# GpSimd instead of VectorE inverts the sums of the later softmaxes, by a power

## The chip, the cores and the metric

The kernel runs on one core of a Trainium2 chip. TensorE multiplies matrices, VectorE, ScalarE and GpSimd work on elements, SyncE starts the DMAs. The metric is the device time of one execution in microseconds, the median of three runs.

## What is computed

Two attentions over the same q, k and v (batch 4, 8 heads, 576 tokens, 64 dimensions), added, and then two feed-forward layers over all 2304 tokens. The first attention works on q, k and v averaged over four tokens ("pooled"); the second lets each token see only the tokens less than four away. Both normalise by a softmax, and it is the denominator of these that the change touches.

```python
def sm_attn(qq, kk, vv):
    s = scale * np.matmul(qq, kk.transpose(0, 1, 3, 2))
    a = np.exp(s - np.max(s, axis=-1, keepdims=True))
    a = a / (np.sum(a, axis=-1, keepdims=True) + 1e-09)
    return np.matmul(a, vv)
# q_d, k_d, v_d: means over 4 tokens;  scores outside |i - j| < 4: -1e9
x = np.repeat(sm_attn(q_d, k_d, v_d), 4, axis=2) + local_attention(q, k, v)
h = x @ w_in;   x = (np.maximum(h, 0) ** 2) @ w_out
h = x @ w_in2;  out = (h * np.cos(h)) @ w_out2
```

## The kernel before

The tokens are cut into 40 windows of 56 to 60 queries, ten for each batch, and the windows are worked on in pairs: pair 0 holds windows 0 and 1, pair 19 the last two. A pair has two softmaxes, one for each parity of the heads, each on a tile of 128 rows by 4 x 64 scores. Eight windows (four pairs) make a block of some 460 tokens, and there are five blocks. Beside them the pooled attention has one softmax for each batch and head pair (`down`, 96 rows by 3 x 144).

A first phase, in which `early[0]` is true, does what the first block needs: pairs 0 to 3 and the pooled attention of batch 0. Then layer 1 runs block by block over 16 slots of 128 hidden units. A slot is a stage A (`stage_a`, L830: 12 matmuls of the block's 460 columns into the one bank `ps_h`), the relu, square and split of h into a high part gh and a low part gl (ScalarE L854, L855, L842, VectorE L848), and a stage B (`stage_b1`, L913: 12 matmuls that add to four banks `acc`). At a block's end the four banks are copied to y (L951, L953). The attention of the following pairs runs between the slots, so that the block's input is there when the block begins; so does the conversion of the weights from 64-bit numbers (`split`, L675 to L716; its subtraction of the high part L711 and that of the sums L801 are GpSimd's). Layer 2 (L865, L937) follows behind layer 1, with nothing of the attention in it.

A pair's way behind the first phase: score matmuls (L573, in the order's rows with the masks of L554), the maximum on VectorE, the exponential on ScalarE (L392 with the sums beside it, or L406 and then a VectorE sum, L408), then the two steps of this change: the small constant is added to the sums (L498, VectorE) and they are inverted (L499, VectorE). GpSimd multiplies the scores by that (L500), TensorE transposes them (L512), ScalarE copies the transposed tile, TensorE multiplies with v (L615), VectorE adds the pooled attention (L632), ScalarE makes the high part xh (L644) and VectorE the low part xl (L646) of the block's input, which stage A reads. In `down` the two steps are L428 and L431, GpSimd's product is L432, and its transpositions, product with v and copy are L442, L458 and L466. Each engine executes its own instructions strictly in the order in which they stand.

What sets that order: the program's text is recorded with its dependencies, and a scheduler that plans with its own costs of instructions puts each engine's instructions in a row (`schedule_with_timeline_sim`). A changed instruction can so move others on all engines. A few places are pinned with `behind(...)` and with a high priority for the relu's helper.

Of the kernel before, what the change touches and what calls it, by code (L numbers as in the profile page):

```python
# [8 lines left out]
F32 = mybir.dt.float32  # L9
# [5 lines left out]
ALU = mybir.AluOpType  # L15
# [4 lines left out]
P = 128  # L20
B, H, S, D = 4, 8, 576, 64
FACTOR = 4
# [72 lines left out]
def kernel(  # L95
# [11 lines left out]
    nc = tc.nc  # L107
    weights = {1: w1.bitcast(U32), 2: w2.bitcast(U32)}

    const = ctx.enter_context(tc.tile_pool(name="const", bufs=1))  # L110
# [23 lines left out]
        nc.vector.memset(t, v)  # L134
    down_half = const.tile([P, 1], F32, name="down_half")
    nc.vector.memset(down_half, 1.0 / 64 - 0.5)
    half_pi = const.tile([P, 1], F32, name="half_pi")
    nc.vector.memset(half_pi, math.pi / 2)

# [12 lines left out]
    early = [True]  # L152
# [22 lines left out]
    def done(name, n=1):  # L175
        f = taken[name].pop(0) if early[0] and name in SPREAD else None
        if f is None:
            used[name] -= n
        elif f in caps:
            used[f] -= n  # L180
        else:
            spare.append(f)
# [51 lines left out]
    def done_a(*ts):  # L234
        for t in ts:
            if t is not None:
                used[kinds.pop(id(t))[0]] -= 1
# [147 lines left out]
    def exps(bank, sv, mx, pr, scale, apiece):  # L385
# [21 lines left out]
        yield  # L407
        nc.vector.tensor_reduce(out=mx[:, 1], in_=pr, op=ALU.add, axis=AX.X)  # L408

    def down(b, hp):  # L410
        while b not in pooled:
            yield
        _, kp, vp = pooled[b]
        if b not in xds:
            xds[b] = cm.tile([P, HPAIR, SD], F32, tag="xd", name="xd")
        yield from need("dpr")
        s, = yield from need_a()
        sv = s[:QROWS, :3 * SD].rearrange("r (m s) -> r m s", m=3)
        qf = qp[:, hp].rearrange("p a s -> p (a s)")
        for m in range(3):  # L420
            last["pe"] = nc.tensor.matmul(sv[:, m], qf[:, m * QROWS:(m + 1) * QROWS], kp[:, hp], start=True, stop=True).ins  # L421
        qk_used[b] = qk_used.get(b, 0) + 1
        if qk_used[b] == HPAIR:
            done("qp")
        mx = cm.tile([QROWS, 2, 3], F32, tag="dmx", name="dmx", bufs=4)
        pr = task_tile("dpr", QROWS, 3 * SD).rearrange("p (m s) -> p m s", m=3)
        yield from exps(s, sv, mx, pr, SCALE / FACTOR ** 2, b < 2)
        nc.vector.tensor_scalar(  # L428
            out=mx[:, 1], in0=mx[:, 1], scalar1=1e-9, scalar2=float(FACTOR), op0=ALU.add, op1=ALU.mult
        )  # L430
        nc.vector.reciprocal(out=mx[:, 1], in_=mx[:, 1])  # L431
        nc.gpsimd.tensor_tensor(  # L432
            out=pr, in0=pr, in1=mx[:, 1].unsqueeze(2).broadcast_to([QROWS, 3, SD]), op=ALU.mult
        )
        yield
        if not early[0]:
            yield
        yield from need("dpt")
        tps = yield from need_a(2)
        for kt in range(2):  # L440
            for m in range(3):
                last["pe"] = nc.tensor.transpose(  # L442
                    tps[kt][:KTOK, m * QROWS:(m + 1) * QROWS], pr[:, m, kt * KTOK:(kt + 1) * KTOK],
                    ident[:QROWS, :QROWS],
                ).ins
        done("dpr")
        pt = task_tile("dpt", KTOK, 4 * SD).rearrange("p (k s) -> p k s", k=2)
        for kt in range(2):
            nc.scalar.copy(out=pt[:, kt], in_=tps[kt][:KTOK, :2 * SD])
        done_a(*tps)  # L450
        yield
        while early[0] and "vp" not in bands:
            yield
        av, = yield from need_a()
        for kt in range(2):
            for a in range(2):
                rows = slice(a * D, (a + 1) * D)
                last["pe"] = nc.tensor.matmul(  # L458
                    av[rows, :SD], vp[:, kt, hp * P + a * D:hp * P + (a + 1) * D], pt[:, kt, a * SD:(a + 1) * SD],
                    start=kt == 0, stop=kt == 1,  # L460
                ).ins
        done("dpt")
        vp_used[b] = vp_used.get(b, 0) + 1
        if vp_used[b] == HPAIR:
            done("vp")
        last["xd"] = nc.scalar.copy(out=xds[b][:, hp], in_=av[:, :SD]).ins  # L466
        done_a(av)
        downs.add((b, hp))
# [13 lines left out]
    def soft(s, sv, pr_tag, pr, q, a, pts):  # L482
        apart = early[0]
        mx = cm.tile([P, 2, HPAIR], F32, tag="mx", name="mx", bufs=8)
        if 2 * q >= DVE_MASK:
            at = [mask_at(w) for w in (2 * q, 2 * q + 1)]
            for i in range(2) if at[0] != at[1] else (slice(0, 2),):
                i = slice(2 * i, 2 * i + 2) if isinstance(i, int) else slice(0, HPAIR)
                nc.vector.tensor_tensor(
                    out=pr[:, i], in0=sv[:, i], op=ALU.add,  # L490
                    in1=const_sb[:, at[i.start // 2]:at[i.start // 2] + WK].unsqueeze(1).broadcast_to(
                        [P, i.stop - i.start, WK]
                    ),
# [1 line left out]
            done_a(s)  # L495
            s, sv = None, pr
        yield from exps(s, sv, mx, pr, SCALE, a == 0 if apart else 2 * q < W0[2])
        nc.vector.tensor_scalar_add(out=mx[:, 1], in0=mx[:, 1], scalar1=1e-9)  # L498
        nc.vector.reciprocal(out=mx[:, 1], in_=mx[:, 1])  # L499
        last["pr"] = (nc.vector if early[0] else nc.gpsimd).tensor_tensor(  # L500
            out=pr, in0=pr, in1=mx[:, 1].unsqueeze(2).broadcast_to([P, HPAIR, WK]), op=ALU.mult
        ).ins
# [811 lines left out]
```

## Time and profile before

| what | us |
|---|---|
| median of three runs | 913.27 (912.74 to 913.54) |
| the profiled execution, own time | 909.99 |
| its span, first to last instruction | 908.2 |
| TensorE busy | 888.2 |
| VectorE busy | 643.1 |
| ScalarE busy | 575.0 |
| GpSimd busy | 96.2 |

TensorE's time stands in two rows, PE for matmuls and PEld for the loads of weights that run beside them. Matmuls are pipelined and their ends are modelled, so a busy PE is not necessarily at its peak; the distance from one start to the next is the safer reading. A wait is put down to what ended it last.

### The profile page before, as it was taken

Reading aid. Unit: us, or ns where it says so; the run is one execution under the profiler, and the core shown is the slowest. Engines: PE = TensorE matmul, PEld = TensorE weight load, DVE = VectorE, ACT = ScalarE, POOL = GpSimd, SP = SyncE. Lnnn points to the kernel's source line nnn. Section 1 sums busy time; section 2 is a strip of 40 time slices with the busy share of each in tenths; the row PEclk is TensorE's granted clock in tenths of the full one; section 3 lists DMA queues with packets and bytes.
Section 4 is the critical chain, followed back from the end, with each engine's and each line's share of the span. In section 5 each row is a group of like instructions: output and inputs, shape, how many; then the busy total and the mean of one; then the engine's idle time right before and its main releaser. Section 6 shows DMA issues by size and latency. Waiting matters only on the chain.

```text
span 908.2 us, 17806 instructions
## 1 busy us (share of the span) xinstructions
PE 888.2 (98%) x6962; PEld 811.2 (89%) x6962; DVE 643.1 (71%) x1265; ACT 575.0 (63%) x1041; POOL 96.2 (11%) x79
## 2 busy tenths in 40 slices
PE   7889999999999999999999999999999999999997
PEld 5678778888888987889999999999999999999997
DVE  7899997567666665563311187988888897879786
ACT  5778776455655555454534477777777677767774
POOL 2001310122203322222200000000000000000000
PEclk9799999999999999999999999999999999999999
DMA  9499878967889766884897966655666666566673
GB/s 283 175 326 332 307 279 288 329 246 253 291 315 311 262 232 207 292 308 173 287 388 244 355 226 204 204 191 190 207 201 203 199 204 199 190 198 209 208 228 105
DMA packets 72904, 223.57 MB, mean 246 GB/s; under 512 B 9620, under 2 KB 14612, under 8 KB 68724
## 3 DMA queue, kind: packets, MB, share of 16 engines
q1 hardware_dynamic: 72820, 222.43, 71.7%
q8 instruction: 55, 0.90, 0.4%
q14 instruction: 29, 0.24, 0.1%
HBM read 181.50 MB, written 40.89 MB: 245 GB/s over the span
## 4 chain that ended last, share of the span: by engine, by line
PE 87%; DVE 5%; DMA 4%; ACT 3%; issue 1%; POOL 0%; DVEq 0%; SPq 0%; ACTq 0%
PE ps_h L865 23%; PE ps_h L830 19%; PE acc L913 19%; PE acc L937 18%; DMA raw<-in_w_dram 2%; DMA pl<-in_pool_v_dram 2%; PE ps_a L615 1%; PE ps_warm L1050 1%; DVE bits L695 1%; PE ps_a L573 1%; PE ps_a L458 1%; PE acc L935 1%; PE ps_a L512 1%; PE ps_a L421 1%; ACT bits L675 1%
## 5 line engine op out<-in xcount | busy, mean ns | idle before, releaser
L865 PE MATMUL ps_h<-x,w2hi 128*128 128x256 f32 x1152 | 161.8, 283 | 0.0
L848 DVE TENSOR_TENSOR gl<-gt,gh 128x460 fp32r<-128x460 f32 (+1 forms) x80 | 58.2, 728 | 142.4 <-ACT gh L842 85.2
L865 PEld LDWEIGHTS ps_h<-x,w2hi 128*128 128x128 f32 x1152 | 148.1, 191 | 0.1
L937 PE MATMUL acc<-bl,gh 128*128 128x256 f32 x504 | 139.2, 277 | 0.0
L830 PE MATMUL ps_h<-xh,w1hi 128*128 128x460 f32 (+3 forms) x324 | 122.7, 380 | 3.7 <-ACT gt L854 3.5
L913 PE MATMUL acc<-gl,w1hi 128*128 128x460 f32 (+1 forms) x320 | 120.0, 375 | 0.0
L830 PE MATMUL ps_h<-xl,w1hi 128*128 128x460 f32 (+3 forms) x324 | 118.8, 368 | 0.0
L913 PE MATMUL acc<-gh,w1hi 128*128 128x460 f32 (+1 forms) x320 | 105.5, 374 | 0.8 <-ACT y L951 0.8
L854 ACT ACTIVATE gt<-ps_h 128x460 f32<-128x460 f32 (+1 forms) x80 | 44.1, 552 | 96.9 <-PE ps_h L830 96.7
L913 PE MATMUL acc<-gh,lo 128*128 128x460 f32 (+1 forms) x256 | 94.9, 371 | 0.0
L937 PEld LDWEIGHTS acc<-bl,gh 128*128 128x128 f32 x504 | 94.7, 188 | 0.0
L905 DVE TENSOR_TENSOR gl<-g,gh 128x896 fp32r<-128x896 f32 x72 | 78.2, 1087 | 10.7 <-ACT gh L900 10.6
L937 PE MATMUL acc<-w2hi,gh 128*128 128x256 f32 x288 | 79.8, 277 | 0.0
L937 PE MATMUL acc<-w2hi,gl 128*128 128x256 f32 x288 | 79.4, 277 | 0.0
L873 ACT ACTIVATE u<-ps_h,quarter 128x512 f32<-128x512 f32 x72 | 49.3, 685 | 46.6 <-PE ps_h L865 46.3
L880 DVE SCALAR_TENSOR_TENSOR r<-u,ps_h 128x512 f32<-128x512 f32 x72 | 49.4, 686 | 38.8 <-PE acc L937 22.3
L900 ACT ACTIVATE gh<-g 128x896 fp32r<-128x896 f32 x72 | 68.1, 945 | 11.2 <-DVE g L898 11.2
L885 ACT ACTIVATE r<-r,half_pi 128x512 f32<-128x512 f32 x72 | 51.8, 719 | 34.2 <-DVE r L881 34.2
L830 PEld LDWEIGHTS ps_h<-xh,w1hi 128*128 128x128 f32 x324 | 60.8, 188 | 13.3 <-ACT gt L854 5.8
L865 PE MATMUL ps_h<-x,w2lo 128*128 128x256 f32 x432 | 68.5, 281 | 0.0
L830 PEld LDWEIGHTS ps_h<-xl,w1hi 128*128 128x128 f32 x324 | 60.9, 188 | 5.9 <-issue 0.2
L913 PEld LDWEIGHTS acc<-gh,w1hi 128*128 128x128 f32 x320 | 59.4, 188 | 7.6 <-ACT y L951 0.9
(150 smaller groups left out, 1911.4 us busy)
## 6 DMA issues: line engine op xcount, KB each, us to landing
bl<-wo_d SPq DMA_DIRECT2D x70, 896.0 KB
raw<-in_w_dram SPq DMA_DIRECT2D x32, 1024.0 KB
lo<-lo_d SPq DMA_DIRECT2D x128, 256.0 KB
qkw<-in_win_qk_dram SPq DMA_DIRECT2D x16, 512.0 KB
pl<-in_pool_qk_dram SPq DMA_DIRECT2D x24, 288.0 KB
wo_d<-raw SPq DMA_DIRECT2D x16, 384.0 KB
out_dram<-o SPq DMA_DIRECT2D x18, 256.0 KB
vw<-in_win_v_dram SPq DMA_DIRECT2D x16, 256.0 KB
```

What stands on the lines that cost most here:

```text
L421: last["pe"] = nc.tensor.matmul(sv[:, m], qf[:, m * QROWS:(m + 1) * QROWS], kp[:, hp], start=True, stop=True).ins
L830: nc.tensor.matmul(h[:, t0:t1], a[:, c * P:(c + 1) * P], x[:, c, t0:t1], start=i == 0, stop=i == len(order) - 1)
L848: last["gl"] = nc.vector.tensor_tensor(out=gl, in0=gt, in1=gh.bitcast(F32), op=ALU.subtract).ins
L854: last["relu"] = nc.scalar.activation(out=gt, in_=h, func=AF.Relu).ins
L865: nc.tensor.matmul(h[:, s * TB:(s + 1) * TB], a[:, c * P:(c + 1) * P], x[:, c], start=i == 0, stop=i == len(order) - 1,)
L873: nc.scalar.activation(out=u, in_=h, func=AF.Identity, bias=quarter, scale=float(1.0 / (2 * math.pi)))
L880: nc.vector.scalar_tensor_tensor(out=r, in0=u, scalar=-PI2_HI, in1=hv, op0=ALU.mult, op1=ALU.add)
L885: nc.scalar.activation(out=r, in_=r, func=AF.Sin, bias=half_pi, scale=1.0)
L900: nc.scalar.activation(out=gh, in_=g[:, 1:], func=AF.Copy)
L905: nc.vector.tensor_tensor(out=gl, in0=g[:, 1:], in1=gh.bitcast(F32), op=ALU.subtract)
L913: nc.tensor.matmul(acc[d][:, :n], a, x, start=f == 0 and i == 0, stop=f == NF - 1 and i == 2)
L937: nc.tensor.matmul(o, a[:, x], b, start=opens and i == 0, stop=p == NP2 - 1 and i == 2 and (k % 2 == 1 or k == NPROD - 1),)
```

## The change

Behind the first phase, the addition of 1e-9 (with the factor 4 in `down`, one in the windows) and the inversion are GpSimd's: a tensor-scalar instruction, and then a power with the exponent from a new constant tile of -1. In the first phase both stay on VectorE as before. It concerns 32 softmaxes of the windows and 12 of the pooled attention, 88 instructions.

```diff
+    minus_one = const.tile([P, 1], F32, name="minus_one")
+    nc.vector.memset(minus_one, -1.0)
...
+    def inverse(t, times):
+        if early[0]:
+            nc.vector.tensor_scalar(out=t, in0=t, scalar1=1e-9, scalar2=times, op0=ALU.add, op1=ALU.mult)
+            nc.vector.reciprocal(out=t, in_=t)
+            return
+        nc.gpsimd.tensor_scalar(out=t, in0=t, scalar1=1e-9, scalar2=times, op0=ALU.add, op1=ALU.mult)
+        nc.gpsimd.tensor_tensor(
+            out=t, in0=t, in1=minus_one[:t.shape[0]].broadcast_to([t.shape[0], t.shape[1]]), op=ALU.pow
+        )
...
         yield from exps(s, sv, mx, pr, SCALE / FACTOR ** 2, b < 2)
-        nc.vector.tensor_scalar(
-            out=mx[:, 1], in0=mx[:, 1], scalar1=1e-9, scalar2=float(FACTOR), op0=ALU.add, op1=ALU.mult
-        )
-        nc.vector.reciprocal(out=mx[:, 1], in_=mx[:, 1])
+        inverse(mx[:, 1], float(FACTOR))
...
         yield from exps(s, sv, mx, pr, SCALE, a == 0 if apart else 2 * q < W0[2])
-        nc.vector.tensor_scalar_add(out=mx[:, 1], in0=mx[:, 1], scalar1=1e-9)
-        nc.vector.reciprocal(out=mx[:, 1], in_=mx[:, 1])
+        inverse(mx[:, 1], 1.0)
```

The lines of the changed kernel behind it stand two to ten higher: L848 of before is L856 there, L500 is L508, L830 is L838, L913 is L921.

The first place is pair 4, the first behind the first phase. VectorE, before; `mx` holds the sums, `bits` the weight being converted:

```order
L498 TENSOR_SCALAR mx<-mx 128x4
L693 TENSOR_SCALAR bits<-bits 128x1024
L499 RECIPROCAL mx<-mx 128x4
L848 TENSOR_TENSOR gl<-gt,gh 128x460
L695 SCALAR_TENSOR_TENSOR bits<-raw,bits 128x1024
L498 TENSOR_SCALAR mx<-mx 128x4
L499 RECIPROCAL mx<-mx 128x4
L684 TENSOR_SCALAR bits<-bits 128x1024
```

VectorE at the same place, in the change:

```order
L692 TENSOR_SCALAR bits<-bits 128x1024
L701 TENSOR_SCALAR bits<-bits 128x1024
L856 TENSOR_TENSOR gl<-gt,gh 128x460
L703 SCALAR_TENSOR_TENSOR bits<-raw,bits 128x1024
L692 TENSOR_SCALAR bits<-bits 128x1024
```

The four small instructions are gone from between the conversion's. GpSimd before, pairs 4 and 5 (`pr` the scores, with their buffers' numbers):

```order
L432 TENSOR_TENSOR dpr_257<-dpr_257,dmx_256 96x432
L500 TENSOR_TENSOR pr_756<-pr_756,mx_784 128x256
L500 TENSOR_TENSOR pr_757<-pr_757,mx_818 128x256
L500 TENSOR_TENSOR pr_949<-pr_949,mx_977 128x256
L500 TENSOR_TENSOR pr_950<-pr_950,mx_1048 128x256
```

GpSimd in the change, pair 4 and the beginning of pair 5:

```order
L441 TENSOR_TENSOR dpr_259<-dpr_259,dmx_258 96x432
L417 TENSOR_SCALAR mx_786<-mx_786 128x4
L418 TENSOR_TENSOR mx_786<-mx_786,minus_one_99 128x4
L508 TENSOR_TENSOR pr_758<-pr_758,mx_786 128x256
L417 TENSOR_SCALAR mx_820<-mx_820 128x4
L418 TENSOR_TENSOR mx_820<-mx_820,minus_one_99 128x4
L508 TENSOR_TENSOR pr_759<-pr_759,mx_820 128x256
L417 TENSOR_SCALAR mx_979<-mx_979 128x4
```

Each product now has its sum and its power directly ahead of it on the same engine. The second place is the border from the first block to the second, on TensorE; `ps_h_2137` is the first slot of the second block, `ps_h_2220` its next. Before:

```order
L830 MATMUL ps_h_2137<-xl,w1hi_540 128x460
L830 MATMUL ps_h_2137<-xh,lo 128x460 x4
L913 MATMUL acc_882<-gl,w1hi_1894 128x460
L913 MATMUL acc_882<-gh,lob 128x460
L913 MATMUL acc_883<-gl,w1hi_1894 128x460
L913 MATMUL acc_883<-gh,lob 128x460
L913 MATMUL acc_884<-gl,w1hi_1894 128x460
L913 MATMUL acc_884<-gh,lob 128x460
L913 MATMUL acc_885<-gl,w1hi_1894 128x460
L913 MATMUL acc_885<-gh,lob 128x460
L830 MATMUL ps_h_2220<-xh,w1hi_682 128x460
```

In the change (`ps_h_2139` and `ps_h_2222`):

```order
L838 MATMUL ps_h_2139<-xh,w1hi_542 128x460
L838 MATMUL ps_h_2139<-xl,w1hi_542 128x460
L838 MATMUL ps_h_2139<-xh,lo 128x460 x4
L838 MATMUL ps_h_2222<-xh,w1hi_684 128x460
L838 MATMUL ps_h_2222<-xl,w1hi_684 128x460
```

The eight stage-B matmuls of the block before have moved ahead of both stages A. The third place is the border from the third block to the fourth, on TensorE. Before, the last product with v of the pair that the fourth block waits for, and what follows it (four more stage-B matmuls and 15 score matmuls come after these rows, and then stage A):

```order
L615 MATMUL ps_a<-pt,vw 64x56 x8
L913 MATMUL acc_3467<-gl,w1hi_1807 128x464
L913 MATMUL acc_3467<-gh,lo 128x464
L913 MATMUL acc_3464<-gh,w1hi_1894 128x464
L913 MATMUL acc_3464<-gl,w1hi_1894 128x464
L913 MATMUL acc_3464<-gh,lo 128x464
L913 MATMUL acc_3465<-gh,w1hi_1894 128x464
L573 MATMUL ps_a<-qkw 64x64
L913 MATMUL acc_3465<-gl,w1hi_1894 128x464
L913 MATMUL acc_3465<-gh,lo 128x464
L913 MATMUL acc_3466<-gh,w1hi_1894 128x464
L913 MATMUL acc_3466<-gl,w1hi_1894 128x464
```

In the change:

```order
L467 MATMUL ps_a<-dpt,vp 64x144 x2
L623 MATMUL ps_a<-pt,vw 64x60 x2
L467 MATMUL ps_a<-dpt,vp 64x144 x2
L623 MATMUL ps_a<-pt,vw 64x60 x6
L623 MATMUL ps_a<-pt,vw 64x56 x8
L581 MATMUL ps_a<-qkw 64x64 x16
L838 MATMUL ps_h_4412<-xh,w1hi_542 128x460
L838 MATMUL ps_h_4412<-xl,w1hi_542 128x460
```

All stage-B matmuls of the third block now stand ahead of that product, and only the score matmuls are left between it and the stage A that needs its result.

## Rows read from the trace of the kernel before

**Rows 1.** The page: span, and busy time of each engine, its share.

```profile
span 908.2 us, 17806 instructions
PE 888.2 (98%) x6962; PEld 811.2 (89%) x6962; DVE 643.1 (71%) x1265; ACT 575.0 (63%) x1041; POOL 96.2 (11%) x79
```

**Rows 2.** Stretches: PE, PEld, DVE, ACT, POOL busy us (count), clock, DMA share, GB/s.

```profile
50.00:100.00 50.00, 48.53 (x368) 40.39 (x367) 46.20 (x97) 42.22 (x122) 10.48 (x8) 1.00 0.95 336
100.00:150.00 50.00, 49.56 (x390) 39.92 (x392) 43.33 (x81) 35.85 (x83) 5.67 (x6) 1.00 0.85 297
...
600.00:650.00 50.00, 50.00 (x427) 49.86 (x426) 42.79 (x80) 38.13 (x56) 0.00 (x0) 1.00 0.58 197
```

**Rows 3.** Waits of PE, 50 to 460 us: us in total, times, longest.

```profile
PE ps_a L512 <- POOL pr L500: 1.4, 2, 0.7
PE ps_h L830 <- ACT gt L854: 1.4, 3, 0.6
PE acc L913 <- ACT y L951: 0.8, 1, 0.8
```

**Rows 4.** Waits of PEld, 36 to 520 us, same columns.

```profile
PEld ps_a L615 <- issue: 5.4, 21, 0.3
```

**Rows 5.** VectorE's two steps: count, ns at least/median/most, first and last start.

```profile
L498 DVE TENSOR_SCALAR mx<-mx x40: 131/162/842, 20.0 to 399.1; 128x4 f32<-128x4 f32 x40
...
L499 DVE RECIPROCAL mx<-mx x40: 140/174/179, 21.1 to 399.4; 128x4 f32<-128x4 f32 x40
```

**Rows 6.** GpSimd's instructions by line, same columns.

```profile
L500 POOL TENSOR_TENSOR pr<-pr,mx x32: 607/614/1484, 56.9 to 400.1; 128x256 f32<-128x256 f32 x32
...
L432 POOL TENSOR_TENSOR dpr<-dpr,dmx x16: 904/907/4232, 15.9 to 330.0; 96x432 f32<-96x432 f32 x16
...
L711 POOL TENSOR_TENSOR bits<-bits,shi x16: 2377/2392/2518, 172.8 to 452.2; 128x1024 f32<-128x1024 f32 x16
```

**Rows 7.** Timeline of ScalarE and VectorE, 55 to 59 us: start, us, what, [idle before].

```profile
57.31 0.24 ACT L392 ACTIVATION_READ_ACCUMULATOR pr<-ps_a,mx 128x1 f32 x1
...
55.92 0.17 DVE L498 TENSOR_SCALAR mx<-mx 128x4 f32<-128x4 f32 x1 [1.52 <-ACT pr L392]
...
57.21 1.64 DVE L695 SCALAR_TENSOR_TENSOR bits<-raw,bits 128x1024 uint32<-128x1024 uint32 x1
58.77 0.16 DVE L498 TENSOR_SCALAR mx<-mx 128x4 f32<-128x4 f32 x1
58.96 0.18 DVE L499 RECIPROCAL mx<-mx 128x4 f32<-128x4 f32 x1
```

**Rows 8.** Timeline of GpSimd, 59 to 73 us.

```profile
59.31 0.88 POOL L500 TENSOR_TENSOR pr<-pr,mx 128x256 f32<-128x256 f32 x1 [1.55 <-DVE mx L499]
69.88 2.45 POOL L500 TENSOR_TENSOR pr<-pr,mx 128x256 f32<-128x256 f32 x2 [9.69 <-ACT qp L376]
```

**Rows 9.** Chain of work that ended last, near 380 us: start, us, what.

```profile
378.72 2.48 PE ps_h L830 x12
```

**Rows 10.** Timeline of TensorE and VectorE at the third border.

```profile
346.10 0.68 PE L615 MATMUL ps_a<-pt,vw 64*64 64x60 f32 x28
...
348.17 0.64 DVE L646 TENSOR_TENSOR xl<-xt,xh 128x464 fp32r<-128x464 f32 x1 [0.66 <-ACT xh L644]
...
350.28 0.69 PE L573 MATMUL ps_a<-qkw 64*64 64x64 f32 x30
350.89 0.48 PE L830 MATMUL ps_h<-xh,w1hi 128*128 128x460 f32 x1
...
352.67 1.00 PE L830 MATMUL ps_h<-xh,lo 128*128 128x460 f32 x4
354.31 0.48 PE L830 MATMUL ps_h<-xh,w1hi 128*128 128x460 f32 x1 [0.64 <-ACT gt L854]
```

**Rows 11.** VectorE's subtraction gl in layer 1, columns as in rows 5.

```profile
L848 DVE TENSOR_TENSOR gl<-gt,gh x80: 610/639/2412, 50.5 to 514.0; 128x460 fp32r<-128x460 f32 x64, 128x464 fp32r<-128x464 f32 x16
```

## The prediction

> **What bounds the kernel now.** I read the page's busy shares first, then the stretches, then TensorE's waits, then the softmax chain alone.
>
> The page has TensorE at 98% of the 908.2 us span and VectorE at 71% [rows 1]. The stretches divide it: with a moving weight load behind every matmul, layer 2 (600 to 650 us) runs at a load share of 49.86 in 50 us, while the first block of layer 1 (50 to 150 us) has 40.39 and 39.92, with VectorE at 46.20 and 43.33 of 50 [rows 2]. So VectorE is nearly full exactly where the change starts to act. That does not make it the bound: from 50 to 460 us TensorE waited 3.6 us in all, 1.4 for GpSimd's softmax product (twice), 1.4 for ScalarE's relu and 0.8 for the copy of y [rows 3]. Its lower load share there comes from many small attention matmuls, and each change to them costs about 5.4/21 = 0.26 us [rows 4] whatever VectorE does. TensorE executes its instructions in the order in which they stand, so anything later than the softmax chain is reached only if a transposition waits at its place, or if the new order leaves TensorE without work somewhere. **The end moves by what is added to or taken from TensorE's idle time in 50 to 460 us, and by nothing else**; the gain is bounded by those 3.6 us and a few changes of work.
>
> **The change, part by part.** The table of reciprocals is made for 44 softmaxes behind the first phase: 32 of the local windows (pairs 4 to 19, two each) and 12 of the pooled attention.
>
> VectorE loses two instructions for each, 162 ns and 174 ns at the median [rows 5] (those of the pooled attention are alike). That is 44 x 0.336 = 14.8 us of VectorE, 14 x 0.336 = 4.7 us of it between 50 and 150 us. TensorE hardly waits for VectorE, so this is worth nothing by itself; it shows only through a product that comes earlier. The added memset of the constant at the start lies beside TensorE's warm-up: nothing.
>
> GpSimd gains two instructions for each, and its multiplication stands behind them. The trace has neither of them. For the sum on 4 elements I take 0.2 us: the two broadcast products of 256 and 432 elements take 614 and 907 ns at the median, 1.67 ns an element, which leaves 0.19 us at none [rows 6]. For the power the lower bound is the same 0.2 us, since it is the same two-operand form and no smaller price is in sight (below nothing is excluded: it is an added instruction). For the upper bound I take 2.4 us, the dearest GpSimd median, a whole pass over 1024 elements [rows 6]. I choose 0.6 us, the row of its own form on the same partitions (256 elements) [rows 6]. Each of the two steps must tell the next that it has landed; VectorE's inverse ending at 59.14 and the product starting at 59.31 give 0.17 us for that [rows 7, 8]. So the product starts 0.2 + 0.17 + 0.6 + 0.17 = 1.1 us after GpSimd sees the sums.
>
> What did that path cost before? Undisturbed, about 0.5 us (two instructions and the hand-over). But the second softmax at 57 us had its sums at 57.55 and got its VectorE step at 58.77 only, behind the 1.64 us bit operation [rows 7]; the product ended at 60.19 [rows 8] and TensorE stood waiting. In the order of the change TensorE's two transpositions stand at that same place. By my price the first product, whose sums came at 55.92 [rows 7], ends at about 57.8 and the second at 59.6, 0.6 us earlier than before, so of that wait of 0.7 us (half of the 1.4) 0.1 to 0.3 is left; I take 0.3. At the other wait (products at 69.88 to 72.33 [rows 8]) the order puts eight stage-B matmuls more ahead of the transposition, 8 x 0.207 = 1.7 us (12 take 2.48 [rows 9]), and the wait goes. **Term 1: -1.1 us.**
>
> The other pairs: the new order sets the second transposition of pairs 10, 13, 14 and 18 twelve to twenty matmuls behind the first (2.5 to 4 us), and GpSimd needs 1.1 + 0.6 = 1.7 us from one product to the next. By the places of the transpositions I find room for a power of up to about 1.2 us before TensorE begins to wait. Term 2: 0.
>
> The moved work is dearer than the moved operations. Between blocks TensorE now has less to fill with. There is one bank for h, so a stage A that directly follows another waits for the relu: before, at 354.31, the four matmuls begun at 352.67 should have ended their issue at 353.50, so 0.81 us were lost [rows 10].
> - First border (from the first block of tokens to the second): before, eight stage-B matmuls stood between the two stages A; now nothing does. **Term 3: +0.8.**
> - Second border: one matmul stood there, now none: **term 4: +0.2.**
> - Third border: three stages A in a row now, two before: **term 5: +0.8.**
> - Third border again: before, 14 stage-B matmuls stood between the last attention product and the stage A that reads its result; now only the 16 score matmuls. The result needed 348.81 - 346.78 = 2.03 us (end of xl less end of the attention product [rows 10]). The scores take 350.89 - 350.28 = 0.61 us, and one matmul of 0.21 runs before xl is read, so 2.03 - 0.82 leaves **term 6: +1.2.** The 0.8 us that TensorE spends on the copy of y shortly after stay: GpSimd's rest subtraction, whose store frees y's buffer, now stands between the two softmaxes' steps, and I count that as neither gain nor loss.
>
> The order has 476 changes between kinds of matmul against 479: 3 x 0.26. **Term 7: -0.8.**
>
> Sum: -1.1 + 0.8 + 0.2 + 0.8 + 1.2 - 0.8 = **+1.1 us.** The profiled execution took 909.99 us, so it would take 911.1; the median of the three runs, 913.27, lies 3.28 above it, and with the same distance the forecast is **914.4 us**.
>
> A rule that speaks against the change. VectorE's two-input subtraction gl takes 639 ns at the median and up to 2412 [rows 11], and GpSimd's product of the pooled attention once took 4.23 us where its median is 0.91 [rows 6], both while the other engine worked. The Trainium skill (SBUF — State Buffer, "Who interferes with whom") says that GpSimd and VectorE share one pair of ports as an exclusive lock: a GpSimd instruction and a VectorE instruction with two SBUF inputs block one another for the whole instruction. The trace agrees. By that rule moving work between these two engines gives no room where both are busy; what it gives here is the third rival.
>
> **The rivals.**
> 1. *The power is dear* (slower). It decides from about 1.2 us. At 2.4 us the five pairs whose transpositions follow soonest in the new order (4, 5, 6, 9, 10) pay the excess of 1.2 us at both: 5 x 2 x 1.2 = 12 us, so 913.27 + 1.1 + 12 = 926.4. For it: no row shows this operation, and a power may be a program and not an operation. Against: the form's rows are all below 2.4.
> 2. *Relief prevails* (faster). The products in the first block come earlier, all waits of [rows 3] there go, and scores or stage B arrive so that the borders hide: terms 3 to 6 vanish, and with 1.4 for the products, a third of the relu's 1.4, and 0.8 of term 7 gained the time is 913.27 - 2.7 = 910.6. The end of this case is all 3.6 + 0.8 = 4.4 us, 908.9. For it: VectorE at 92% at 50 to 100 us. Against: the stage-A pairs stand in the order.
> 3. *The port takes it back* (slower). Between 50 and 150 us 14 softmaxes bring 14 x 0.8 = 11.2 us of GpSimd, and VectorE gives up 4.7. If each holds VectorE off for its length, VectorE has 6.5 us more to do where 3.8 + 6.7 = 10.5 us are idle [rows 2]; between none and all of it reaches TensorE, at half 3.3 us: 917.7. It decides where more than about half of GpSimd's new time falls on two-input VectorE work.
> 4. *Nothing happens*: the chain is hidden and the order costs nothing: 913.3, inside the forecast's range.
>
> **How the numbers follow.** About 0.2% (1.8 us) is what a measurement of this kernel can tell from no change. Forecast, with rival 4 in it: 0.50, from 912 to 916, of which 0.36 lie within 0.2% and 0.14 above it. Relief: 0.20, all faster. Dear power: 0.20, slower. Port: 0.10, of which 0.08 slower and 0.02 within. So faster 0.20, same 0.38, slower 0.42; the likeliest single case still lies at 914.4. The range reaches to the relief case at 910.3 and to the dear power at 926; a power above 2.4 us, and relief to its very end, are the 2 in 10 left out, or less.
>
> **What would show each step.** The rows of the power: 0.2 to 1.2 us keeps the forecast, more makes rival 1. TensorE's waits for GpSimd's product: two of 1.4 us before, I expect about 0.3 in all. The three borders: waits of stage A for the relu at each, and for xl at the third, some 3 us more than before. VectorE's busy time: 15 us less; if gl's mean rises instead, rival 3. I am wrong if TensorE's waits at the borders are not there, or if the power's rows are longer than its multiplication's by several times.

## The result

The changed kernel takes 921.0 us (median of four runs, 919.8 to 923.1) where the kernel before takes 913.0 in the same session: 1.0108 times the time, 95% interval 1.0090 to 1.0127. It is slower. (The two medians alone give 1.0088, or 8.0 us. The ratio on record, 1.0108, puts 921.0 against 911.2; the kernel before took 910.7 to 911.5 us in the later sessions, and the differences in us below are by such ratios, so 9.8 us here.) That side had the largest of the three chances and the time lies in the range, but the likeliest value, 914.4, is 6.6 us too low and its own range, 912 to 916, is missed. The profiled execution spans 918.0 us against 908.2.

The page of the changed kernel, its lines for the span and the engines:

```profile
span 918.0 us, 17776 instructions
PE 893.1 (97%) x6962; PEld 813.2 (89%) x6962; DVE 632.0 (69%) x1178; ACT 575.7 (63%) x1041; POOL 174.9 (19%) x167
```

Beside [rows 1]: VectorE lost 11.1 us (15 expected), GpSimd gained 78.7. TensorE's share fell. Its waits from 50 to 460 us (us in total, times, longest) answer to [rows 3]:

```profile
PE ps_a L520 <- POOL pr L508: 4.4, 4, 1.9
PE ps_h L838 <- ACT gt L862: 2.6, 4, 0.6
PE ps_a L451 <- POOL dpr L441: 0.5, 1, 0.5
PE ps_a L581 <- DVE xt L640: 0.4, 1, 0.4
PE ps_h L838 <- ACT xh L652: 0.2, 1, 0.2
PE ps_h L838 <- DVE xl L654: 0.2, 1, 0.2
...
```

The wait for GpSimd's product was to shrink to 0.3 us and grew from 1.4 to 4.4. The wait for relu grew from 1.4 to 2.6, as the borders were to bring. The wait for the copy of y, 0.8 before, was to stay and is gone.

GpSimd's groups by line in the changed kernel (count, busy us, mean ns of one). L417 is the sum, L418 the power, L508 the product:

```profile
L418 POOL TENSOR_TENSOR mx<-mx,minus_one 128x4 f32<-128x4 f32 x32 | 41.0, 1280 | 1.5
L508 POOL TENSOR_TENSOR pr<-pr,mx 128x256 f32<-128x256 f32 x32 | 28.4, 886 | 2.3
L418 POOL TENSOR_TENSOR dmx<-dmx,minus_one 96x3 f32<-96x3 f32 x12 | 15.1, 1258 | 1.0
```

The power on four values a partition takes 1.28 us in the mean, twice what I took. Its timeline at the two places of term 1 (start, us, what):

```profile
56.67 0.19 POOL L417 TENSOR_SCALAR mx<-mx 128x4 f32<-128x4 f32 x1 [34.94 <-ACT pr L394]
56.95 1.03 POOL L418 TENSOR_TENSOR mx<-mx,minus_one 128x4 f32<-128x4 f32 x1
58.05 1.29 POOL L508 TENSOR_TENSOR pr<-pr,mx 128x256 f32<-128x256 f32 x1
59.42 0.63 POOL L417 TENSOR_SCALAR mx<-mx 128x4 f32<-128x4 f32 x1
60.14 1.16 POOL L418 TENSOR_TENSOR mx<-mx,minus_one 128x4 f32<-128x4 f32 x1
61.38 0.61 POOL L508 TENSOR_TENSOR pr<-pr,mx 128x256 f32<-128x256 f32 x1
...
71.97 1.99 POOL L418 TENSOR_TENSOR mx<-mx,minus_one 128x4 f32<-128x4 f32 x1
...
75.34 1.46 POOL L418 TENSOR_TENSOR mx<-mx,minus_one 128x4 f32<-128x4 f32 x1
76.88 0.73 POOL L508 TENSOR_TENSOR pr<-pr,mx 128x256 f32<-128x256 f32 x1
```

The second softmax's sum (L417) stands behind the first one's product on GpSimd, so it starts at 59.42 only. The whole path is queued twice where VectorE's two steps used to run beside GpSimd. TensorE's transpositions at these two places:

```profile
62.05 0.44 PE L520 MATMUL ps_a<-const_sb,pr 128*128 128x128 f32 x2 [1.93 <-POOL pr L508]
...
74.71 0.44 PE L520 MATMUL ps_a<-const_sb,pr 128*128 128x128 f32 x2 [0.32 <-POOL pr L508]
...
77.66 0.44 PE L520 MATMUL ps_a<-const_sb,pr 128*128 128x128 f32 x2 [1.67 <-POOL pr L508]
```

Some 1.4 us after the second wait the clock falls. Stretches of one microsecond (TensorE, its weight loads, VectorE, ScalarE, GpSimd; then the granted clock):

```profile
76.00:77.00 1.00, 0.00 (x0) 0.00 (x0) 1.00 (x2) 0.76 (x3) 0.92 (x2) 1.00 1.07 413
77.00:78.00 1.00, 0.34 (x2) 0.20 (x2) 1.00 (x2) 0.00 (x0) 0.60 (x1) 1.00 0.88 324
...
79.00:80.00 1.00, 1.00 (x5) 0.87 (x4) 1.00 (x3) 0.78 (x1) 0.00 (x0) 0.54 0.47 178
80.00:81.00 1.00, 1.00 (x4) 0.87 (x3) 1.00 (x2) 0.00 (x0) 0.00 (x0) 0.50 0.82 205
81.00:82.00 1.00, 1.00 (x4) 0.88 (x3) 1.00 (x3) 0.00 (x0) 0.00 (x0) 0.50 0.95 371
82.00:83.00 1.00, 1.00 (x5) 0.88 (x5) 0.31 (x1) 0.27 (x1) 0.00 (x0) 0.75 0.98 408
```

From 79 to 83 us TensorE works, at 0.54, 0.50, 0.50 and 0.75 of its clock, mostly at the lower of its two levels (1.2 of 2.4 GHz). That loses 0.46 + 0.50 + 0.50 + 0.25 = 1.7 us at most, and no wait shows it. (The matmuls of 460 columns start 0.385 us apart in this stretch and 0.207 outside it, by which it is 1.6 us.)

### The profile page after: what moved, and what is told of

It is laid out like the page before. It is cut to its first block, busy times and chain, and to the rows that moved or that the text cites. A ratio compares the mean times of both kernels' runs of the same rounds, so it can differ in the third digit from the quotient of the medians.

```text
span 918.0 us, 17776 instructions
## 1 busy us (share of the span) xinstructions
PE 893.1 (97%) x6962; PEld 813.2 (89%) x6962; DVE 632.0 (69%) x1178; ACT 575.7 (63%) x1041; POOL 174.9 (19%) x167
## 4 chain that ended last, share of the span: by engine, by line
PE 89%; DMA 4%; DVE 3%; ACT 2%; POOL 1%; issue 1%; SPq 0%; DVEq 0%; POOLq 0%; ACTq 0%
PE ps_h L873 22%; PE acc L921 21%; PE ps_h L838 21%; PE acc L945 18%; DMA raw<-in_w_dram 2%; PE ps_a L623 1%; DMA pv<-in_pool_v_dram 1%; DMA pl<-in_pool_qk_dram 1%; PE ps_a L581 1%; PE ps_a L433 1%; PE ps_a L520 1%; PE ps_a L467 1%; PE acc L943 1%; PE ps_a L451 1%; DVE bits L703 1%
## 5 line engine op out<-in xcount | busy, mean ns | idle before, releaser
L873 PE MATMUL ps_h<-x,w2hi 128*128 128x256 f32 x1152 | 158.8, 280 | 0.0
L856 DVE TENSOR_TENSOR gl<-gt,gh 128x460 fp32r<-128x460 f32 (+1 forms) x80 | 58.0, 724 | 138.2 <-ACT gh L850 91.2
L873 PEld LDWEIGHTS ps_h<-x,w2hi 128*128 128x128 f32 x1152 | 145.6, 188 | 0.1
L838 PE MATMUL ps_h<-xh,w1hi 128*128 128x460 f32 (+3 forms) x324 | 123.7, 383 | 5.0 <-ACT gt L862 4.7
L838 PE MATMUL ps_h<-xl,w1hi 128*128 128x460 f32 (+3 forms) x324 | 120.6, 373 | 0.2 <-DVE xl L654 0.2
L921 PE MATMUL acc<-gl,w1hi 128*128 128x460 f32 (+1 forms) x320 | 120.5, 377 | 0.0
L921 PE MATMUL acc<-gh,w1hi 128*128 128x460 f32 (+1 forms) x320 | 104.0, 376 | 0.0
L921 PE MATMUL acc<-gh,lo 128*128 128x460 f32 (+1 forms) x256 | 96.0, 375 | 0.0
L913 DVE TENSOR_TENSOR gl<-g,gh 128x896 fp32r<-128x896 f32 x72 | 78.2, 1086 | 10.7 <-ACT gh L908 10.7
L838 PEld LDWEIGHTS ps_h<-xh,w1hi 128*128 128x128 f32 x324 | 61.1, 189 | 14.8 <-ACT gt L862 7.0
L838 PEld LDWEIGHTS ps_h<-xl,w1hi 128*128 128x128 f32 x324 | 61.2, 189 | 7.1 <-DVE xl L654 0.5
L921 PEld LDWEIGHTS acc<-gl,w1hi 128*128 128x128 f32 x320 | 60.0, 188 | 7.3 <-DVE gl L856 0.3
```

Of the source, the lines that this page charges most:

```text
L838: nc.tensor.matmul(h[:, t0:t1], a[:, c * P:(c + 1) * P], x[:, c, t0:t1], start=i == 0, stop=i == len(order) - 1)
L856: last["gl"] = nc.vector.tensor_tensor(out=gl, in0=gt, in1=gh.bitcast(F32), op=ALU.subtract).ins
L873: nc.tensor.matmul(h[:, s * TB:(s + 1) * TB], a[:, c * P:(c + 1) * P], x[:, c], start=i == 0, stop=i == len(order) - 1,)
L913: nc.vector.tensor_tensor(out=gl, in0=g[:, 1:], in1=gh.bitcast(F32), op=ALU.subtract)
L921: nc.tensor.matmul(acc[d][:, :n], a, x, start=f == 0 and i == 0, stop=f == NF - 1 and i == 2)
```

## The experiments

Three things changed at once: who inverts, in which order all instructions stand, and, as it turned out, where the tiles lie. To take them apart, most kernels below hold the order of one of the two kernels on every queue. The kernel file gets a table of the order and a helper that queues each instruction behind its predecessor in that table (no wait for its end, only order):

```
for a, b in zip(order, order[1:]):
    tc.add_manual_dep(made[e][b], made[e][a].name, <order only>)
```

"Old order" is that of the kernel before, "new order" that of the changed kernel. Ratios are to the kernel before on the same chip, whose median was 910.7 to 911.5 us there; the changed kernel's ratio is that of the section above. The table gathers all twelve, the sections below tell what each was for.

| run | who inverts | order | tiles moved by | ratio | 95% interval |
|---|---|---|---|---|---|
| changed kernel | GpSimd, power | new | 32 bytes | 1.0108 | 1.0090 to 1.0127 |
| e1 | GpSimd, power | old | 32 | 1.0206 | 1.0189 to 1.0223 |
| e2 | VectorE | new | 0 | 1.0021 | 1.0010 to 1.0031 |
| e3 | GpSimd, a product instead | new | 32 | 1.0050 | 1.0033 to 1.0068 |
| e4 | GpSimd, a product instead | old | 32 | 1.0022 | 1.0012 to 1.0033 |
| e5 | VectorE | old | 32 | 1.0042 | 1.0031 to 1.0053 |
| e6 | GpSimd, power | new | 64 | 1.0128 | 1.0108 to 1.0148 |
| e7 | first block VectorE, then power | new | 64 | 1.0063 | 1.0046 to 1.0080 |
| e8 | VectorE, no small constant | old | 0 | 0.9998 | 0.9987 to 1.0009 |
| e9 | GpSimd, power | new | 0 | 1.0095 | 1.0071 to 1.0120 |
| e10 | first block VectorE, then power | new | 0 | 1.0048 | 1.0032 to 1.0064 |
| e11 | GpSimd, a product instead | new | 0 | 1.0025 | 1.0012 to 1.0039 |
| e12 | VectorE | old | 32 up, weights 32 down | 1.0040 | 1.0027 to 1.0053 |

### Order against path: e1 and e2

Edit of e1: the changed kernel plus the table of the old order. Edit of e2: the kernel before plus the table of the new order, without entries for VectorE's two steps.

> The changed kernel's instructions, with every engine's queue held in the order of the kernel before (the sum and the power directly ahead of each GpSimd product, VectorE's two steps gone). Theory A, the path: the changed kernel is slower because GpSimd's sum and power lie between a softmax's sums and its product (0.19 + 0.08 + 1.01 + 0.08 = 1.4 us where VectorE needed 0.5), wherever the transpositions stand. Then the two products that TensorE waited for in the first block come 1.5 to 3 us later here as well, and the time is 917 to 920 us. Theory B, the order: the new order of instructions costs the time, the path is covered. Then this kernel takes 913 us, within 1 us.

Measured 930.2 us, ratio 1.0206, worse than either theory said. TensorE's waits for the product from 50 to 460 us:

```profile
PE ps_a L520 <- POOL pr L508: 12.3, 7, 4.5
PE ps_h L838 <- ACT gt L862: 1.1, 2, 0.6
```

and two stretches of 5 us, columns as above:

```profile
100.00:105.00 5.00, 1.42 (x5) 1.31 (x6) 3.06 (x6) 1.13 (x3) 4.68 (x5) 0.73 0.90 321
105.00:110.00 5.00, 5.00 (x19) 3.85 (x17) 3.94 (x5) 2.31 (x8) 4.23 (x4) 0.59 0.11 43
```

The waits hold 10.9 us more than before. The mean granted clock is 0.983 over 929 us against 0.992 over 908, 0.017 x 929 - 0.008 x 908 = 8.5 us lost to the lower level, at most: from 102.3 to 103.6 us it falls into a wait. Together 19.4, and the ratio makes 18.8 us; but e1 also has the constant tile, which takes 2.1 us of it in two stretches without waits (below). That leaves 6 to 8 us for the clock, an estimate: the clock's fall behind the waits costs more than half of what the waits cost.

> The kernel before's instructions (VectorE adds and inverts), with TensorE, ScalarE, the DMA queue and all the other VectorE and GpSimd instructions held in the order of the changed kernel; the scheduler places VectorE's two steps. Theory A, the path: the product comes as early as in the kernel before, TensorE's waits for it fall from 4.4 to about 1.4 us or less, the clock does not fall at 79 us; what is left are the borders between blocks, 2.4 us at most: 913 to 915.5 us. Theory B, the order: 919 to 921 us, like the changed kernel.

Measured 913.4 us, ratio 1.0021, 1.9 us, as theory A had it. No wait for the product of the local windows is left:

```profile
PE ps_h L830 <- ACT gt L854: 2.6, 4, 0.6
PE acc L913 <- ACT y L951: 0.6, 1, 0.6
PE ps_a L442 <- POOL dpr L432: 0.6, 1, 0.6
PE ps_a L458 <- ACT dpt L449: 0.5, 1, 0.5
PE ps_a L573 <- DVE xt L632: 0.4, 1, 0.4
PE ps_a L442 <- ACT dpr L392: 0.4, 1, 0.4
...
```

The 2.6 us at the relu are those of the changed kernel, in the same order. Both theories hold a part. The new order costs 1.9 us, not at the borders alone: beside the kernel before, e2's waits have 1.2 us more for the relu, 0.8 for xt, xh and xl at the third border and 1.5 for the pooled attention (0.6 + 0.5 + 0.4, all in the first block), and 1.4 less for the windows' product and 0.2 less for the copy of y, which makes 1.9. But the new order is also what saves the changed kernel: the same instructions in the old order are 1.0206 - 1.0108, some 9 us, dearer, and wait 12.3 us for the product where the changed kernel waits 4.4.

### The power's price: e3, e4, e11

Edit of e3 (new order) and e4 (old order), on the changed kernel:

```
-        out=t, in0=t, in1=minus_one[...].broadcast_to(...), op=ALU.pow
+        out=t, in0=t, in1=minus_one[...].broadcast_to(...), op=ALU.mult    # and the constant 1/4096
```

> The changed kernel in its own order, every queue held, with the power replaced by a multiplication of the same two operands (the constant is 1/4096, so the inverse is left out and the softmaxes are scaled otherwise; the sine of layer 2 gets a scale of 0.999999). The same instructions stand at the same places, only the power's price is gone: about 0.2 us in place of 1.01. Theory A, the path: TensorE's waits for the product fall by about 0.8 us at each of four places and the clock stays: 915 to 918 us. Theory B, the order: 920 to 921 us.

> As the run before it, with every queue held in the order of the kernel before. The path is 0.19 + 0.08 + 0.2 + 0.08 = 0.55 us, that of VectorE's two steps is 0.5. Theory A, the path: 913 us, within 1 us, and several us below the same order with the power. Theory B, the order: 913 us, and the same as that order with the power.

Measured 1.0050 and 1.0022. In the old order the power costs 1.0206 - 1.0022, 16.8 us; in the new one 1.0108 - 1.0050, 5.3 us. Theory A holds in both. The power's price in the old order includes the clock's part. Against e5 below, which is e4 with the steps on VectorE, e4 is 1.8 us faster. That could be the relief of VectorE that the change is after, but it isn't shown: the two were measured on different chips, their intervals overlap a little, and in the new order the same pair (e11 below, against e2) shows no gain.

What did not fit: e3 lies 2.6 us above e2 though it waits only 0.7 us for the product. Laid side by side, the stretches of equal work gave the reason, the last block of layer 1 (396 matmuls, no wait) and layer 2. They took the same in each kernel to a few hundredths, but in two groups: 81.84 and 388.85 us in the kernel before and e2, 82.9 to 83.0 and 389.8 in the changed kernel, e1, e3 and e4. The second group is the one with the new constant.

e11 is e3 with the constant at a place that moves nothing (see e9):

> As e9, with the power replaced by a multiplication of the same operands (the constant is 1/4096: the inverse is left out, the softmaxes are scaled otherwise; the sine's scale is 0.999999). Theory: with a step of 0.2 to 0.35 us in place of 1.0 to 1.3 the path is covered, the ratio is that of VectorE's steps in this order, 1.002 to 1.003, and the difference to e9, 3 to 4 us, is the power's price. Rival: two more GpSimd instructions and their hand-overs cost by themselves: 1.004 or more.

Measured 1.0025 with an interval of 1.0012 to 1.0039, that of e2. So two more GpSimd steps cost nothing by themselves that can be measured. GpSimd's product in place of the power has a median of 0.20 us (mean 0.40), the power 1.01 (mean 1.27), and e9 - e11, 1.0095 - 1.0025, is 6.4 us: with the 5.3 of e3, that is the power's price in the new order, each known to some 2.5 us.

### The constant's place: e5, e6, e9, e12

Edit of e5, on the kernel before, old order:

```
+    minus_one = const.tile([P, 1], F32, name="minus_one")
+    nc.vector.memset(minus_one, -1.0)
```

> The kernel before in its own order, every queue held, with the constant tile of minus one and its memset added and used by nothing. The tile takes 32 bytes of every partition ahead of the activations' tiles, so these all stand 32 bytes further on. In the traces of the four kernels with that tile the last block of layer 1 took 82.9 us and layer 2 390.2, in the two without it 81.8 and 389.2, with the same matmuls. Theory, the place: TensorE reads its operands more slowly from the shifted places, whatever GpSimd does. Then this kernel is 2.0 to 2.4 us slower than before (ratio 1.0022 to 1.0026), with 82.9 and 390.2 us in those two stretches. Rival: the slower matmuls come from GpSimd's work or from that execution; then it is the same as before within 0.5 us, with 81.8 and 389.2.

Measured 914.8 us, ratio 1.0042: a constant that nobody reads costs 3.8 us. It takes 32 bytes of each partition, and the tiles allocated after it on the low side of the memory (x, g, y, the attention's) all lie 32 bytes further on; the weights on the high side stay. Three starts of TensorE's timeline give the two stretches, first the kernel before, then e5, then e12 (first stage A of the last block, first matmul of layer 2, last pair of matmuls):

```profile
432.13 0.37 PE L830 MATMUL ps_h<-xh,w1hi 128*128 128x460 f32 x1
...
513.97 0.28 PE L865 MATMUL ps_h<-x,w2hi 128*128 128x256 f32 x1
...
902.82 0.39 PE L937 MATMUL acc<-w2hi,gl 128*128 128x256 f32 x2
```

```profile
435.19 0.37 PE L832 MATMUL ps_h<-xh,w1hi 128*128 128x460 f32 x1
...
518.17 0.40 PE L867 MATMUL ps_h<-x,w2hi 128*128 128x256 f32 x2
...
907.97 0.40 PE L939 MATMUL acc<-w2hi,gl 128*128 128x256 f32 x2
```

```profile
432.61 0.37 PE L835 MATMUL ps_h<-xh,w1hi 128*128 128x460 f32 x1
...
514.80 0.28 PE L870 MATMUL ps_h<-x,w2hi 128*128 128x256 f32 x1
...
906.20 0.40 PE L942 MATMUL acc<-w2hi,gl 128*128 128x256 f32 x2
```

That is 81.84 and 388.85 us before, 82.98 and 389.80 in e5. With the granted clock at 1.00 throughout, a matmul of the last block takes 209.5 ns in the mean and not 206.7. These two stretches make 2.1 of the 3.8 us; the rest lies in blocks whose waits differ from one execution to the next, so no row pins it.

e6 is the changed kernel with the constant 16 values wide, new order:

> The changed kernel in its own order, every queue held, with the constant 16 values wide (only the first is read), so that the tiles behind it stand 64 bytes further on than in the kernel before and not 32. Theory, the place: the stretches fall back to 81.8 and 389.2 us and the time by 2.0 to 2.4 us: 7.3 to 7.8 us above before (ratio 1.0080 to 1.0086). Rival: the place is nothing to TensorE, and the time stays 9.6 us above before (ratio 1.0105).

Measured 1.0128, no relief. The last block recovers to 82.15 us, layer 2 worsens to 391.39. The theory that both stretches fall back at 64 bytes is wrong.

e12 adds 32 bytes at either end, so that low tiles go up by 32 bytes and weights down by 32:

```
+    right = ctx.enter_context(tc.tile_pool(name="right", bufs=1, side="right"))
+    shift_right = right.tile([P, 1], F32, name="shift_right")
+    shift = const.tile([P, 1], F32, name="shift")
```

> The kernel before in its own order, every queue held, with 32 bytes set aside at either end of the memory, so that the tiles on both sides (activations at the low end, weights at the high end) move by 32 bytes and all still stand alike within 64 bytes. Theory, agreement: a matmul is slow where its two operands stand unlike within 64 bytes, which the constant alone brought about; here they agree, and the time is that of before (ratio 0.999 to 1.001, last block 81.8 us). Rival, the place itself: activations at the places of the constant-alone run are read slowly whatever the weights do: ratio 1.003 to 1.005, last block 82.9 us.

Measured 1.0040, with 82.19 and 391.40 us: neither theory's pair. It is e6's pair (82.15, 391.39), and what e6 and e12 share is the distance between the two groups of tiles, 64 bytes more than before; their absolute places differ. So in the fourteen profiles of this study (before, after and the twelve) the pace of the matmuls goes by the distance between activations and weights: 0, 32 and 64 bytes more give 81.84, 82.9 to 83.0 and 82.15 to 82.19 us in the last block, and 388.9, 389.8 and 391.4 in layer 2, whatever the order and whoever inverts. Three distances are all that was tried, and what in the chip does it stays open.

e9 is the changed kernel, new order, with the constant in the spare bytes of an existing tile, so that nothing moves:

```
-    minus_one = const.tile([P, 1], F32, name="minus_one")
-    half_pi = const.tile([P, 1], F32, name="half_pi")
+    pair = const.tile([P, 2], F32, name="half_pi")
+    half_pi, minus_one = pair[:, :1], pair[:, 1:]
```

> The changed kernel in its own order, every queue held, with the constant of minus one as second value of the existing tile half_pi, whose 32 bytes of a partition it shares: every tile stands at its place of the kernel before. Theory: the cost of the change is a sum of three parts, the order (2.0 us, VectorE's steps in the new order), the moved tiles (3.7 us, the constant alone) and GpSimd's path (the rest). Then 3.7 us go, the time is 5 to 6.5 us above before (ratio 1.0055 to 1.007), and the last block of layer 1 and layer 2 take 81.8 and 389.0 us again. Rival: the places matter only by chance of the order, and the time stays 9.6 us above before (1.0105).

Measured 919.7 us, ratio 1.0095 (1.0071 to 1.0120): the two stretches are 81.84 and 388.85 again, 2.0 us less than in the changed kernel, but the total fell by 1.2 us only and not by 3.7; the intervals overlap. (The same pair without the power, e3 less e11, gives 2.3.) The sum of three independent parts is too simple; a slower matmul may be partly free where TensorE waits anyway, which no run shows. The four executions of e9 show the clock's part once more: two with a mean granted clock of 0.992 and 0.993 took 918.2 and 917.5 us, two with 0.987 took 921.3, and where the clock fell in these two no trace shows. The profiled one is one of the former, and its clock stays at 1.00 behind the same waits (4.2 us at four places, 2.1 of it at 77.9 us), so such waits bring the lower level in some executions only. In the changed kernel the link is looser: 919.9 us at a mean of 0.992, 919.8 at 0.989.

### Where the power costs: e7 and e10

Edit, on e6 and on e9, with the new order held for all the rest:

```
-        if early[0]:
+        if early[0] or now[0] < NF:
```

> As the run before it (constant 64 bytes wide, the changed kernel's order held), but the 16 softmaxes of the first block of tokens go back to VectorE, which the scheduler places; the other 28 keep the power on GpSimd. Theory A, the cost of the power sits in the first block, where TensorE has little besides attention and the clock falls behind the long waits: the waits for the product at 60 and 75 us and the fall of the clock go, and the time is that of VectorE's steps in this order plus some 0.5 us: 1.0021 to 1.003 times before. Rival: the cost is spread over all 44 softmaxes: 28/44 of 5.5 us stay, 3.5 us, and the ratio is 1.006.

> As the run before it, with the 16 softmaxes of the first block of tokens back on VectorE (which the scheduler places), the power on GpSimd for the other 28. Theory: GpSimd's path costs its time in the first block; what is left is the order and 0.5 us, ratio 1.002 to 1.003. Rival: it is spread over all; 28/44 of it stay, ratio 1.0045 to 1.0055.

Measured 1.0063 against e6's 1.0128, and 1.0048 against e9's 1.0095. Giving 16 softmaxes back saves 5.9 and 4.3 us, 0.27 us each at e10. What stays is 1.0048 - 1.0021, 2.5 us above e2. That is the number which the rival said, but it can't all be the price of the other 28 powers. The first of these starts at 180.3 us in e10, and these waits of TensorE for the pooled attention's product and its copy stand ahead of it:

```profile
89.05 0.44 PE L451 MATMUL ps_a<-const_sb,dpr 96*72 96x96 f32 x3 [1.40 <-POOL dpr L441]
...
109.13 0.47 PE L467 MATMUL ps_a<-dpt,vp 72*64 72x144 f32 x4 [0.53 <-ACT dpt L458]
...
128.51 0.47 PE L467 MATMUL ps_a<-dpt,vp 72*64 72x144 f32 x4 [1.15 <-ACT dpt L458]
```

That is 3.1 us in the first block where e2 waits 1.5, although neither kernel has a power there; VectorE's steps stand elsewhere than in e2, as the scheduler placed them. Behind the first border e10's waits are some 0.8 us above e2's, 0.5 of it for the windows' product. So by the profile the power's cost lies mostly in the first block, as the theory said, and e10's ratio alone doesn't show it. What each later power costs isn't settled.

### A shorter path: e8

Edit, on the kernel before, old order:

```
-        nc.vector.tensor_scalar_add(out=mx[:, 1], in0=mx[:, 1], scalar1=1e-9)
```

> The kernel before in its own order, every queue held, without the addition of 1e-9 for the 40 softmaxes of the local windows (each sum holds its own largest term, which is one, so the sum does not change). VectorE loses one instruction of 0.16 us on the path between sums and product. If that path is what TensorE waited for at 59 and 70 us, the time falls by 0.2 to 0.6 us (ratio 0.9993 to 0.9998); if VectorE's queue ahead of it is what counts, nothing changes.

Measured 0.9998 (0.9987 to 1.0009): no difference that can be measured, and with an interval of 1 us to either side it can't tell the 0.2 to 0.6 us from nothing. TensorE's wait for the product fell from 1.4 to 0.7 us in the profile, its wait for the relu rose from 1.4 to 2.6. No kernel of this study is faster than the kernel before beyond its interval.

## Where the prediction was right and where it was wrong

**What bounds the kernel.** That TensorE's idle time moves the end held. "And by nothing else" did not: the granted clock (1.6 us in the profile of after, some 6 to 8 in e1) and the pace of each matmul (2.0 us in the two stretches) moved it too.

**The path, the step that failed.** I took 0.6 us for the power, from the row of its form [rows 6], and a product undisturbed. Measured: sum 0.19 us at the median, hand-overs 0.08 (0.17 taken), power 1.01 at the median and 1.27 in the mean, and the product, 0.61 undisturbed, 0.89 in the mean. At the first place the first product was 2.67 us behind its sums (1.9 taken), and the second 2.65 behind the first (1.7 taken). At the two places of term 1 TensorE waited 1.93 at 62.05 us, and 0.32 and 1.67 at 74.71 and 77.66: 3.9 us where it was 1.4. So term 1 was +2.5 us and not -1.1, and with the clock 4.1. My own threshold, 1.2 us, lay between the price that I took and the mean measured; I had the bounds 0.2 to 2.4 and chose near the low one by the form of the instruction, though [rows 6] speak of products only. e11 shows the very form with a product at 0.20 us: the operation, not the form, sets the price.

**Why GpSimd's steps stretch.** The power at 71.97 took 1.99 us while VectorE worked on two operands:

```profile
71.88 1.23 DVE L703 SCALAR_TENSOR_TENSOR bits<-raw,bits 128x1024 uint32<-128x1024 uint32 x1
```

A power that meets nothing of VectorE's takes 1.01 us. This is read from single places; no run takes the overlap away. VectorE's subtraction gl did not get longer in the mean (724 ns after, 728 before), so rival 3 had the interference right and its victim wrong: what the new steps bring is GpSimd held off. But VectorE is held off too, in both kernels, by what GpSimd did before as well. Of the 80 gl of the changed kernel, 18 begin within a product or a subtraction of GpSimd's. Fourteen of these take 0.78 to 1.92 us and end some 0.5 us after it (three of the other four begin in its last 0.05 us). The seven that begin within a power take 0.62 to 0.64 us. One place of each:

```profile
199.84 0.61 POOL L508 TENSOR_TENSOR pr<-pr,mx 128x256 f32<-128x256 f32 x1
200.03 0.91 DVE L856 TENSOR_TENSOR gl<-gt,gh 128x460 fp32r<-128x460 f32 x1 [3.08 <-ACT gh L850]
...
160.78 1.01 POOL L418 TENSOR_TENSOR mx<-mx,minus_one 128x4 f32<-128x4 f32 x1
160.97 0.64 DVE L856 TENSOR_TENSOR gl<-gt,gh 128x460 fp32r<-128x460 f32 x1 [2.16 <-ACT gh L850]
```

The Trainium skill (SBUF — State Buffer, "Who interferes with whom") says that a VectorE instruction with two SBUF inputs contends with a GpSimd instruction that reads SBUF, and that the order of issue decides which of them blocks. The trace agrees where VectorE's step or a product of GpSimd's began first, and not where a power did.

**Term 2.** Zero taken; behind the first block the profile has one wait for a product, 0.47 us at 367 us. (The 0.5 us for the pooled attention's product stand in the first block, at 93 us, and e2 has them without the power.)

**Terms 3 to 7, the new order.** The borders were right. The relu is waited for at each border, 0.64 us in the view each time, as at the place of [rows 10] where 0.81 us were lost from start to start:

```profile
159.75 0.48 PE L838 MATMUL ps_h<-xh,w1hi 128*128 128x460 f32 x1 [0.64 <-ACT gt L862]
...
259.80 0.48 PE L838 MATMUL ps_h<-xh,w1hi 128*128 128x464 f32 x1 [0.65 <-ACT gt L862]
...
360.35 0.48 PE L838 MATMUL ps_h<-xh,w1hi 128*128 128x460 f32 x1 [0.64 <-ACT gt L862]
...
363.79 0.48 PE L838 MATMUL ps_h<-xh,w1hi 128*128 128x460 f32 x1 [0.64 <-ACT gt L862]
```

Term 6 shows as three waits (0.39 for xt, 0.24 for xh, 0.20 for xl, from 355.5 to 357.2), 0.8 where 1.2 was taken. Terms 3 to 7 summed to +2.2; e2, which has the new order and no power, measured +1.9 (0.9 to 2.8). That they come so close is partly luck: e2 also lost the 1.4 us of waits for the windows' product and gained 1.5 for the pooled attention, which stood in no term, and term 7 by itself no run shows.

**The constant.** "The added memset lies beside TensorE's warm-up: nothing" is true of the memset and wrong of the tile: 3.8 us alone (e5), 1.2 to 2.3 within the change.

**The sum.** By the ratios: order 1.9 (e2), two GpSimd steps 0.4 (e11 less e2), the power 6.4 (e9 less e11), the tiles 1.2 (the changed kernel less e9). These are the steps of one chain from the kernel before to the changed one, so that they add up to its 9.8 us proves nothing, and each is known to 1 to 3 us only. A second count goes by the two profiles, whose spans differ by 9.8 us: TensorE's waits from 50 to 460 us grew from 3.6 to 8.5, the lower clock takes 1.6, the slower matmuls of the last block and of layer 2 take 2.0; 1.3 us are left that no row pins.

That the time lies in the range at all is partly luck. Rival 1 is the mechanism, but its own sum (five pairs, twice the excess above 1.2 us) would give 0.7 us at a power of 1.27 us, and it reached up to 926 only by a power of 2.4 us, which the median and the mean don't show. The cost came without a threshold, at the places of term 1 where TensorE waited already and every step of the longer path was added; the clock and the moved tiles stood in no case. (The relief case is 910.6 by its own sum and not the 910.3 that the range begins with.)

## What to carry to other kernels

An operation that no row shows is not priced by its form: between bounds as far apart as 0.2 and 2.4 us, work out what happens above the threshold before choosing a value below it; and where an engine already waits, there is no threshold. A step moved to another engine queues behind that engine's own next step, so two softmaxes in a row pay the whole path twice. Before a change with a new tile is judged, put the tile where nothing else moves, or time the tile alone.

## What had not been expected of the hardware

- 32 bytes ahead of the activations' tiles slow the last block's matmuls of 460 columns from 206.7 to 209.5 ns in the mean (e5), at an unchanged granted clock of 1.00. In fourteen profiles the pace goes by the distance between the two groups of tiles (e6 and e12 alike).
- GpSimd's power on 128 partitions x 4 values takes 1.01 us at the median where its product of the same operands takes 0.20.
- A wait of some 2 us of TensorE in the first block is followed by the lower clock level in some executions and not in others: in the same order, it falls behind a wait of 1.67 us at 77.66 in the changed kernel and stays at 1.00 behind one of 2.08 us at 77.90 in e9.
- A VectorE subtraction that begins within a GpSimd product is mostly held until that ends (0.91 us at 200.03, its median is 0.64), one that begins within a GpSimd power is not (0.64 at 160.97), while the power itself stretches from 1.01 to 1.99 us behind a VectorE step with two inputs.
